# First layer about the mean, for batches 1 to 3: GpSimd products and VectorE sums in place of one-column TensorE products

## The chip, the cores and the metric

The kernel runs on one core of a Trainium2 chip. The metric is the time of one execution on the device in microseconds (us), lower is better. The core's engines run beside each other, each through its own list of instructions in order: TensorE (PE; its weight loads are shown as PEld), VectorE (DVE), ScalarE (ACT), GpSimd (POOL) and SyncE (SP), which only issues transfers. GpSimd issues transfers too.

## The reference

```python
def _attn_ref(q, kv, w_sr):                 # q (4, 12288, 128), kv (4, 384, 32, 128)
    kv_pool = kv.reshape(B, H // 4, 4, W // 4, 4, C).mean(axis=(2, 4))
    kv_flat = kv_pool.reshape(B, -1, C) @ w_sr          # 768 keys, k = v
    s = (q @ kv_flat.transpose(0, 2, 1)) / np.sqrt(C)
    a = np.exp(s - s.max(-1, keepdims=True))
    a /= a.sum(-1, keepdims=True) + 1e-09
    return a @ kv_flat

def _moe_ref(x, w_in, w_out):               # x (49152, 128), w_in (128, 2048), w_out (2048, 128)
    h = x @ w_in
    return (h - np.tanh(h)) @ w_out
```

The attention's output, 4 batches of 12288 tokens, is the x of the second function. Everything is fp32.

## The kernel before

**Rounds.** Each batch has 24 *rounds* of 512 tokens, so there are 96, numbered from 0; each has the same work. The hidden layer is developed about one point for each batch: the mean of its keys times w_sr (the *centre*). The point's own hidden values are worked out once for each batch, and the rounds then carry only each token's distance from the centre.

In a round TensorE issues 3 pairs of scores (L850), 3 pairs of values (L894), 2 sums of the softmax shares (L878, `x<-rs,share`; this one is used below as the mark of a round), 3 products for the linear term of q (L884) and 3 for that of the distance (L954), 8 pairs of the hidden layer (L965, `big<-dr,winr`) and 8 pairs back into the result (L1003, `acc<-r,Wr`). Each of the 8 results in `big` is turned into a cube. For seven, ScalarE squares (L969) and VectorE multiplies (L972). For the eighth ScalarE copies it (L976), and GpSimd makes the cube by three instructions over 128x1024: z+ (L979), z* (L983, `z<-z,v`) and rp (L983, `rp<-z,v`). The last pair back of each round is the one from rp (L1003, `acc<-rp,Wr`). ScalarE takes the three exponentials (L854), VectorE multiplies them (L857). GpSimd also rounds the distance (dr L908) and its rest (dl L934), the rest of q (ql L888), and issues two adding transfers (L873) that sum three tiles r into rs, from which L878 reads.

**Preparing a later batch.** While a batch runs, the next is prepared between its instructions. The names below are those of the code. First 15 adding transfers from GpSimd (*gathers*, L437; one more, the first, comes from SyncE) pool the batch's keys into one tile kvp (128x768). VectorE sums kvp in six parts (L502) and makes the mean of them (L506, L507). ScalarE subtracts the mean (L511); TensorE makes the centre, one column (L514), VectorE copies it to `col` (L517). Then `first(n)`, for n from 0 to 3, is four products of a 128x128 block of the fp32 weights with that column (L614, `x<-col,win`), and `take_first(n)` on VectorE copies the four columns into `hb` (L619), which holds a number for each of the 2048 hidden units as 128x16. From hb GpSimd works out three chains of small instructions: first order (L639 to L646), slopes (L650 to L656), third order (L665 to L670). After these come the scaled weights of the batch, all on GpSimd: winr (L714, 4 instructions of 128x512), Wr (L776, 4) and Wg (L756, 4), and one small instruction each for Mh and Ah. On TensorE there are also the products of keys and values (L521, L530), a moment (L547) and four blocks of slopes (L763, `x<-Wg,wout`). The batch 0 is prepared before its first round, with the same functions in other forms.

**The order.** Every instruction of every engine is put in order ahead of time by a class `Plan`: it walks a clock, and on each engine issues what is ready in the order of a *step* (8 steps are a round), using a rough cost for each instruction. The table `MOVES` shifts the steps of single pieces of the preparation, the table `AT` sets those of the pieces of a round. The costs set only the order; the chip then runs it in that order, each engine waiting where an operand or a buffer is not ready. Buffers are rings by tag: `kc` has 2 (used for keys, then for the scales of winr), `A` has 2, `rs` has 3, `rp` 2.

## Time and profile before

| | us |
|---|---|
| three runs | 1289.19, 1290.86, 1291.06 |
| median | 1290.86 |
| the profiled execution's own time | 1289.32 |
| its span (first to last instruction) | 1287.6 |
| busy share | PE 98%, DVE 94%, ACT 93%, POOL 89% |

The profile is of one execution: its span is that from the first instruction to the last. A row of the timeline has the start, the time from issue to end, the engine, line, tiles, shape and count, and in brackets how long the engine stood idle before it and what it waited for. Where instructions of an engine overlap (TensorE's always, GpSimd's when they are queued), what one of them costs is the distance from start to start, not the second column.

### The profile page before, as it was taken

To read this page: it belongs to the slowest core of one execution; us is meant where nothing else is said; L and a number is where in the kernel's file an instruction comes from. 1 tells how busy PE (TensorE), PEld (TensorE's weight loads), DVE (VectorE), ACT (ScalarE), POOL (GpSimd) and SP (SyncE) were. 2 spreads that over 40 slices of the span, in tenths; PEclk is the share of its full clock that TensorE was granted. 3 is DMA by queue.
4 is the path that set the end of the run, shared out by engine and by line. 5 is a ranking of instruction groups with operands and counts; after the bars stand their busy time and mean duration, and the time that the engine had idled before them with its cause. 6 is when DMAs were issued, how large, how long until landed. Compare 5 with 4: busy or idle time off the path is not lost.

```text
span 1287.6 us, 17375 instructions
## 1 busy us (share of the span) xinstructions
PE 1257.1 (98%) x5520; PEld 879.8 (68%) x5520; DVE 1213.7 (94%) x1201; ACT 1201.0 (93%) x1423; POOL 1147.5 (89%) x969
## 2 busy tenths in 40 slices
PE   5899999999999999999999999999999999999997
PEld 4666667777676677777766667776776666666665
DVE  6899899999999999999999999999999999999996
ACT  4799999999999999999999999999999999999995
POOL 3599987999999988899999987899988988989886
PEclk8999999999999999999999999999999999999999
DMA  9367744456657543455467743444434444344431
GB/s 364 69 144 151 167 98 107 111 127 148 143 132 161 120 118 90 125 131 138 108 148 143 160 103 103 103 119 107 115 90 115 103 106 118 93 115 103 106 88 33
DMA packets 82708, 158.46 MB, mean 123 GB/s; under 512 B 9937, under 2 KB 12113, under 8 KB 82609
## 3 DMA queue, kind: packets, MB, share of 16 engines
q0 software_dynamic: 33552, 66.99, 30.7%
q1 hardware_dynamic: 49056, 90.29, 20.0%
q8 instruction: 45, 0.74, 0.2%
q14 instruction: 55, 0.44, 0.1%
HBM read 57.93 MB, written 25.39 MB: 65 GB/s over the span
## 4 chain that ended last, share of the span: by engine, by line
PE 74%; POOL 14%; DMA 4%; issue 2%; DVE 2%; ACT 2%; SPq 0%; POOLq 0%; ACTq 0%; DVEq 0%
PE big L965 23%; PE acc L1003 22%; PE big L850 8%; PE x L894 8%; PE acc L954 4%; PE x L884 4%; DMA rs<-r 3%; POOL rp L983 3%; PE x L878 3%; POOL z L983 2%; POOL z L979 2%; POOL rs L873 2%; POOL ql L888 1%; POOL dl L934 1%; DVE r L972 1%
## 5 line engine op out<-in xcount | busy, mean ns | idle before, releaser
L972 DVE SCALAR_TENSOR_TENSOR r<-big,u 128x1024 fp32r<-128x1024 f32 x672 | 788.7, 1218 | 26.8 <-ACT u L969 26.4
L969 ACT ACTIVATE u<-big 128x1024 f32<-128x1024 f32 x672 | 671.1, 1029 | 34.8 <-PE big L965 23.3
L965 PE MATMUL big<-dr,winr 128*128 128x512 f32 x1536 | 518.9, 419 | 0.7 <-DVE r L972 0.6
L1003 PE MATMUL acc<-r,Wr 128*128 128x512 f32 x1344 | 414.5, 398 | 0.6 <-DVE r L972 0.6
L857 DVE SCALAR_TENSOR_TENSOR r<-E,big 128x1024 f16<-128x1024 f32 x288 | 350.2, 1217 | 22.5 <-ACT E L854 21.8
L965 PEld LDWEIGHTS big<-dr,winr 128*128 128x128 f32 x1536 | 272.1, 188 | 118.8 <-DVE r L972 33.0
L854 ACT ACTIVATE E<-big 128x1024 f32<-128x1024 f32 x288 | 297.2, 1033 | 3.7 <-PE big L850 2.5
L1003 PEld LDWEIGHTS acc<-r,Wr 128*128 128x128 f32 x1344 | 250.0, 188 | 58.5 <-DVE r L972 1.5
L983 POOL TENSOR_TENSOR rp<-z,v 128x1024 fp32r<-128x1024 f32 x96 | 270.8, 2821 | 0.2
L983 POOL TENSOR_TENSOR z<-z,v 128x1024 f32<-128x1024 f32 x96 | 243.8, 2539 | 0.1
L873 POOL DMA_DIRECT2D rs<-r x188 | 211.2, 1124 | 7.6 <-DMA rs<-r 6.1
L979 POOL TENSOR_SCALAR z<-v 128x1024 f32<-128x1024 f32 x96 | 122.7, 1278 | 82.1 <-ACT v L976 81.8
L850 PE MATMUL big<-qr,kTr 128*128 128x512 f32 x576 | 193.0, 417 | 0.4 <-ACT winr L746 0.2
L888 POOL TENSOR_TENSOR ql<-q,qr 128x512 fp32r<-128x512 f32 x96 | 185.2, 1929 | 1.1 <-ACT qr L835 1.1
L894 PE MATMUL x<-r,vvr 128*128 128x512 f16 x576 | 174.3, 385 | 0.0
L934 POOL TENSOR_TENSOR dl<-df,dr 128x512 fp32r<-128x512 f32 x96 | 163.2, 1700 | 0.0
L850 PEld LDWEIGHTS big<-qr,kTr 128*128 128x128 f32 x576 | 101.4, 188 | 39.9 <-DVE r L972 21.9
L976 ACT COPY v<-big 128x1024 f32<-128x1024 f32 x96 | 97.5, 1016 | 8.1 <-PE big L965 1.6
L894 PEld LDWEIGHTS <-vvr 128*128 128x128 f16 x576 | 33.4, 98 | 78.6 <-issue 78.4
L908 POOL TENSOR_SCALAR dr<-df 128x512 fp32r<-128x512 f32 x96 | 81.4, 848 | 0.0
L1003 PE MATMUL acc<-rp,Wr 128*128 128x512 f32 x192 | 77.0, 482 | 3.6 <-POOL rp L983 3.6
L1014 ACT ACTIVATE o<-acc,At 128x512 f32<-128x512 f32 x96 | 65.6, 683 | 7.5 <-PE acc L1003 7.4
(184 smaller groups left out, 1029.9 us busy)
## 6 DMA issues: line engine op xcount, KB each, us to landing
rs<-r POOLq DMA_DIRECT2D x188, 256.0 KB, 3.6
q<-in_q_dram SPq DMA_DIRECT2D x96, 256.0 KB
out_dram<-o SPq DMA_DIRECT2D x96, 256.0 KB
rs<-r SPq DMA_DIRECT2D x94, 256.0 KB
kvp<-in_kv_by_place_dram POOLq DMA_DIRECT2D x45, 384.0 KB, 6.0
r<-in_kv_by_key_dram SPq DMA_DIRECT2D x6, 512.0 KB
kc<-inverse SPq DMA_DIRECT2D x12, 256.0 KB
u<-in_moe_w_in_dram SPq DMA_DIRECT2D x3, 512.0 KB
```

Source lines behind the costliest of these rows:

```text
L850: PE.matmul(out=half(plan[s], h), lhsT=plan[kTr][:, n * P : (n + 1) * P], rhs=plan[qr], start=True, stop=True)
L854: A.activation(out=plan[e], in_=plan[s], func=AF.Exp)
L857: V.scalar_tensor_tensor(out=plan[r], in0=plan[e], scalar=-1.0, in1=plan[s], op0=ALU.add, op1=ALU.subtract)
L873: PL.dma_start(out=plan[rs], in_=plan[r2s[k]], accum_op=ALU.add)
L888: PL.tensor_tensor(out=plan[ql], in0=plan[qs], in1=plan[qr].bitcast(F32), op=ALU.subtract)
L894: PE.matmul(out=plan[num], lhsT=plan[vvr][:, n], rhs=half(plan[f"r2.{g}.{k}"], h), start=(start and h == 0), stop=(stop and h == 1))
L934: PL.tensor_tensor(out=plan[dl], in0=plan[df], in1=plan[dr].bitcast(F32), op=ALU.subtract)
L965: PE.matmul(out=half(plan[hp], h), lhsT=plan[winr][:, f * P : (f + 1) * P], rhs=plan[dr], start=True, stop=True)
L969: A.activation(out=plan[u], in_=plan[hp], func=AF.Square)
L972: V.scalar_tensor_tensor(out=plan[r], in0=plan[hp], scalar=1.0, in1=plan[u], op0=ALU.add, op1=ALU.mult)
L983: PL.tensor_tensor(out=plan[to], in0=plan[x], in1=plan[y], op=ALU.mult)
L1003: PE.matmul(out=plan[acc], lhsT=plan[Wr][:, 2 * n + h], rhs=half(plan[r], h), start=(start and h == 0), stop=(stop and h == 1))
```

## The change

For the batches 1 to 3:

- The centre is made in another form: a product of 128x128 with the mean broadcast as weights, so that every partition holds the whole centre; ScalarE scales it into a tile of tag `A`.
- `first(n)` is one GpSimd product, 128x512: the transposed weights of four blocks by the centre, into a tile of tag `kc`. `take_first(n)` is a sum on VectorE over 128 columns, four times (128x4x128 to 128x4).
- The keys' mean is one sum on VectorE over 768 columns in place of six partial ones and a sum.
- The planner's cost of a gather and of an adding transfer goes from 0.88 and 0.9 to 0.62, their delays to landing from 2.3 and 1.43 to 2.5 and 1.5. The tables MOVES (now with nearly every piece of the preparation, and new entries `taken` for take_first) and AT have new numbers throughout.

```diff
     MOVES = {
-        "load.i.0": -22.9, "load.i.1": -18.7, "words.i.1": -54.5, "words.i.3": -7.3, "WW": -172.2,
+        "load.i.0": -587.048, "words.i.0": -199.957, "load.i.1": -193.024, "words.i.1": 138.935,
...
-            plan.op(put - (0.01 if w else 4), *(("POOL", 0.88) if w else ("SP", 0.5)), gather, (), (kvp,),
-                    late=0.81 if w else 1.0, dma=2.3 if w else 1.1)
+            plan.op(put - (0.01 if w else 4), *(("POOL", 0.62) if w else ("SP", 0.5)), gather, (), (kvp,),
+                    late=0.81 if w else 1.0, dma=2.5 if w else 1.1)
...
-        sb(cen, "col", [P, 1])
+        sb(cen, *(("A", [P, C]) if b else ("col", [P, 1])))
...
-            V.tensor_reduce(out=r[:, 24:25], in_=r[:, 0:24], op=ALU.add, axis=AX.X)
+            V.tensor_reduce(out=r[:, 24:25], in_=plan[kvp] if b else r[:, 0:24], op=ALU.add, axis=AX.X)
...
-            PE.matmul(out=plan[pc][:, 0:1], lhsT=wsr, rhs=plan[row][:, 25:26], start=True, stop=True)
+            mean_of = plan[row][:, 25:26]
+            if b:
+                PE.matmul(out=plan[pc][:, 0:P], lhsT=mean_of.to_broadcast([P, P]), rhs=wsr, start=True,
+                          stop=True)
...
+                A.activation(out=plan[cen], in_=plan[pc][:, 0:P], func=AF.Copy, scale=-1.0 / W)
...
-        for n in range(NK // 2):
+        for n in range(0 if b else NK // 2):
...
         def first(n):
-            for k in range(4):
-                f = 4 * n + k
-                at = plan[f"{ph}.{n}"][:, k : k + 1] if b else plan[f"{ph}.0"][:, f : f + 1]
-                PE.matmul(out=at, lhsT=win32[:, f * P : (f + 1) * P], rhs=plan[cen], start=True,
+            if b:
+                by = plan[cen].unsqueeze(1).to_broadcast([P, FT // 4, C])
+                PL.tensor_tensor(out=plan[f"{ph}.{n}"], in0=winT[:, 4 * n : 4 * n + 4], in1=by, op=ALU.mult)
+                return
...
         def take_first(n):
-            to, of = (slice(4 * n, 4 * n + 4), slice(0, 4)) if b else (slice(0, FT),) * 2
-            V.tensor_scalar(out=x(0)[:, to], in0=plan[f"{ph}.{n}"][:, of], scalar1=1.0, scalar2=None,
-                            op0=ALU.mult)
+            if b:
+                V.tensor_reduce(out=x(0)[:, 4 * n : 4 * n + 4], in_=plan[f"{ph}.{n}"], op=ALU.add, axis=AX.X)
...
     AT = dict(
-        forth=[4.5, 6.4, 3.4, 2.2, 5.4, 5.7, 0.3, 2.8],
+        forth=[6.183, 7.436, 3.897, 1.231, 6.907, 6.934, 0.646, 2.941],
...
-                plan.op(s0 + AT["added"][k - 1], "POOL", 0.9, partial(added, k), (r2s[k],), to,
-                        late=0.81, dma=1.43, lane=True)
+                plan.op(s0 + AT["added"][k - 1], "POOL", 0.62, partial(added, k), (r2s[k],), to,
+                        late=0.81, dma=1.5, lane=True)
```

In the order of before, TensorE has this around the first of the four blocks for batch 2 (L514 makes the centre, L614 are the one-column products):

```order
L1003 MATMUL acc_5000<-r_4942,Wr_2762 128x512 x2
L514 MATMUL x_5030<-row_4601,wsr_66 128x1
L965 MATMUL big_5032<-dr_4883,winr_3208 128x512 x2
L1003 MATMUL acc_5000<-r_4957,Wr_2762 128x512 x2
L614 MATMUL x_5043<-col_5037,win32_67 128x1 x4
L1003 MATMUL acc_5000<-r_4981,Wr_2762 128x512 x2
L965 MATMUL big_5057<-dr_5023,winr_3208 128x512 x2
```

In the order of after (L1009, L1047, L998 are the lines of before 965, 1003, 954) TensorE has for the same batch only the centre, L542:

```order
L998 MATMUL acc_5651<-dl_5599,Ah_3906 128x512
L1009 MATMUL big_5661<-dr_5535,winr_3156 128x512 x2
L1047 MATMUL acc_5651<-r_5580,Wr_2620 128x512 x2
L1009 MATMUL big_5672<-dr_5535,winr_3156 128x512 x2
L1047 MATMUL acc_5651<-r_5591,Wr_2620 128x512 x2
L1009 MATMUL big_5682<-dr_5535,winr_3156 128x512 x2
L1047 MATMUL acc_5651<-r_5608,Wr_2620 128x512 x2
L542 MATMUL x_5689<-wsr_66,row_4310 128x128
L1047 MATMUL acc_5651<-r_5632,Wr_2620 128x512 x2
L1009 MATMUL big_5697<-dr_5670,winr_3156 128x512 x2
```

Four blocks like the first are gone from TensorE for each of three batches, and nothing has come in their place there.

GpSimd in the order of before, in the round in which the first chain of batch 2 runs (the chain starts at L639):

```order
L983 TENSOR_TENSOR z_5572<-z_5572,v_5559 128x1024
L873 DMA rs_5555<-r2_5581 128x1024
L983 TENSOR_TENSOR rp_5622<-z_5572,v_5559 128x1024
L934 TENSOR_TENSOR dl_5647<-df_5574,dr_5585 128x512
L873 DMA rs_5555<-r2_5561 128x1024
L888 TENSOR_TENSOR ql_5674<-q_5234,qr_5470 128x512
L639 TENSOR_TENSOR hb_5060<-hb_5060 128x16
L640 TENSOR_SCALAR hb_5060<-hb_5060 128x16
```

In the order of after, GpSimd has the products (L649) of batch 2 in these places (L1023, L952, L1027, L917, L978, L932 are 979, 908, 983, 873, 934, 888 of before; L679 starts the first chain):

```order
L932 TENSOR_TENSOR ql_5757<-q_5331,qr_5558 128x512
L649 TENSOR_TENSOR kc_5770<-winT_68,A_5695 128x512
L1023 TENSOR_SCALAR z_5809<-v_5796 128x1024
L952 TENSOR_SCALAR dr_5822<-df_5811 128x512
L1027 TENSOR_TENSOR z_5809<-z_5809,v_5796 128x1024
L649 TENSOR_TENSOR kc_5850<-winT_68,A_5695 128x512
L649 TENSOR_TENSOR kc_5858<-winT_68,A_5695 128x512
L649 TENSOR_TENSOR kc_5868<-winT_68,A_5695 128x512
L917 DMA rs_5792<-r2_5827 128x1024
L1027 TENSOR_TENSOR rp_5889<-z_5809,v_5796 128x1024
L679 TENSOR_TENSOR hb_5816<-hb_5816 128x16
L680 TENSOR_SCALAR hb_5816<-hb_5816 128x16
```

Three of the four products stand between z* and the adding transfer and rp of one round (round 39; for batch 3 it is round 63, in the same pattern; for batch 1 all four stand in round 12), and the first chain follows rp there.

GpSimd early in batch 0, where the gathers (L437) for batch 1 run, in the order of before:

```order
L437 DMA kvp_342<-in_kv_by_place_dram 128x768
L873 DMA rs_1020<-r2_1048 128x1024
L983 TENSOR_TENSOR rp_1100<-z_1041,v_1026 128x1024
L934 TENSOR_TENSOR dl_1127<-df_1039,dr_1052 128x512
L437 DMA kvp_342<-in_kv_by_place_dram 128x768
L873 DMA rs_1020<-r2_1028 128x1024
L888 TENSOR_TENSOR ql_1165<-q_716,qr_937 128x512
L979 TENSOR_SCALAR z_1178<-v_1161 128x1024
```

And in that of after (L463 is the gather):

```order
L917 DMA rs_744<-r2_770 128x1024
L1027 TENSOR_TENSOR rp_809<-z_761,v_748 128x1024
L978 TENSOR_TENSOR dl_838<-df_763,dr_774 128x512
L917 DMA rs_744<-r2_750 128x1024
L932 TENSOR_TENSOR ql_859<-q_295,qr_661 128x512
L463 DMA kvp_312<-in_kv_by_place_dram 128x768
L1023 TENSOR_SCALAR z_897<-v_884 128x1024
```

Before had two gathers in each of four early rounds, each gather ahead of one of the round's adding transfers; after has one a round there, behind the last of them, and doubles only later.

## Rows read from the trace of the kernel before

**Rows 1.** The page's busy times; columns: us, share of the span, instructions.

```profile
PE 1257.1 (98%) x5520; PEld 879.8 (68%) x5520; DVE 1213.7 (94%) x1201; ACT 1201.0 (93%) x1423; POOL 1147.5 (89%) x969
```

**Rows 2.** Timeline of TensorE, 1100 to 1128: start, time, instruction, [idle, releaser].

```profile
1112.19 0.60 PE L878 MATMUL x<-rs,share 128*128 128x512 f16 x2
...
1115.35 0.82 PE L1003 MATMUL acc<-rp,Wr 128*128 128x512 f32 x2
...
1124.51 0.61 PE L878 MATMUL x<-rs,share 128*128 128x512 f16 x2
```

**Rows 3.** Timeline of TensorE, 459 to 487, a block of products for batch 2.

```profile
473.19 0.60 PE L878 MATMUL x<-rs,share 128*128 128x512 f16 x2
...
483.13 0.95 PE L614 MATMUL x<-col,win 128*128 128x1 f32 x8
...
486.35 0.61 PE L878 MATMUL x<-rs,share 128*128 128x512 f16 x2
```

**Rows 4.** Groups by line: count | busy us, mean ns | idle.

```profile
L502 DVE TENSOR_REDUCE row<-kvp 128x4 f32<-128x128 f32 x24 | 6.3, 276 | 2.5 <-POOL kvp L460 2.5
...
L466 DVE TENSOR_REDUCE kvp<-E 128x64 f32<-128x1024 f32 x2 | 2.4, 1214 | 0.0
...
L732 POOL TENSOR_TENSOR Wg<-ident,hb 128x512 f32<-128x512 f32 x2 | 2.1, 1042 | 4.9 <-ACT E L854 4.9
...
L732 DVE TENSOR_TENSOR Wg<-ident,hb 128x512 f32<-128x512 f32 x2 | 1.3, 682 | 0.0
...
L619 DVE TENSOR_SCALAR hb<-x 128x4 f32<-128x4 f32 x12 | 1.8, 151 | 0.0
```

**Rows 5.** Timeline of GpSimd, 600 to 640, among winr, Wr and a gather.

```profile
613.71 2.87 POOL L983 TENSOR_TENSOR z<-z,v 128x1024 f32<-128x1024 f32 x1
...
622.20 2.61 POOL L714 TENSOR_TENSOR winr<-win,kc 128x512 fp32r<-128x512 f32 x1
623.70 1.96 POOL L437 DMA_DIRECT2D kvp<-in_kv_by_place_dram  x1
...
626.83 2.85 POOL L983 TENSOR_TENSOR z<-z,v 128x1024 f32<-128x1024 f32 x1
...
636.82 2.07 POOL L776 TENSOR_TENSOR Wr<-wout,hb 128x512 fp32r<-128x512 f32 x1
637.83 2.07 POOL L979 TENSOR_SCALAR z<-v 128x1024 f32<-128x1024 f32 x1
...
639.99 2.87 POOL L983 TENSOR_TENSOR z<-z,v 128x1024 f32<-128x1024 f32 x1
```

**Rows 6.** Timeline of GpSimd, 526 to 560, the slopes chain.

```profile
535.72 0.20 POOL L650 TENSOR_SCALAR hb<-hb 128x16 f32<-128x16 f32 x1
...
537.76 1.04 POOL L756 TENSOR_TENSOR Wg<-winT,hb 128x512 f32<-128x512 f32 x1
```

**Rows 7.** Timeline of GpSimd, 1100 to 1126, no preparation left.

```profile
1111.39 2.67 POOL L983 TENSOR_TENSOR rp<-z,v 128x1024 fp32r<-128x1024 f32 x1
...
1119.06 1.05 POOL L979 TENSOR_SCALAR z<-v 128x1024 f32<-128x1024 f32 x1 [1.60 <-ACT v L976]
```

**Rows 8.** Timeline of TensorE, 523 to 541, the products of keys for batch 2.

```profile
524.94 0.60 PE L878 MATMUL x<-rs,share 128*128 128x512 f16 x2
...
539.80 0.60 PE L878 MATMUL x<-rs,share 128*128 128x512 f16 x2
```

**Rows 9.** Waits of all engines: us in total, times, longest.

```profile
PEld acc L1003 <- POOL rp L983: 7.9, 12, 1.6
```

**Rows 10.** Timeline of GpSimd, 110 to 154, two gathers in a round.

```profile
123.59 1.20 POOL L437 DMA_DIRECT2D kvp<-in_kv_by_place_dram  x1
...
137.24 1.19 POOL L437 DMA_DIRECT2D kvp<-in_kv_by_place_dram  x1
```

**Rows 11.** Timeline of TensorE, 48 to 62, ahead of the first round's hidden layer.

```profile
57.90 2.05 PE L763 MATMUL acc<-Wg,wout 128*128 128x129 f32 x16 [0.70 <-DVE wout L355]
59.70 1.19 PE L965 MATMUL big<-dr,winr 128*128 128x512 f32 x4
```

More of the change, by code (lines that the diff above doesn't have):

```diff
@@ L610, in first @@
         def first(n):
-            for k in range(4):
-                f = 4 * n + k
-                at = plan[f"{ph}.{n}"][:, k : k + 1] if b else plan[f"{ph}.0"][:, f : f + 1]
-                PE.matmul(out=at, lhsT=win32[:, f * P : (f + 1) * P], rhs=plan[cen], start=True,
+            if b:
+                by = plan[cen].unsqueeze(1).to_broadcast([P, FT // 4, C])
+                PL.tensor_tensor(out=plan[f"{ph}.{n}"], in0=winT[:, 4 * n : 4 * n + 4], in1=by, op=ALU.mult)
+                return
+            for f in range(4 * n, 4 * n + 4):
+                PE.matmul(out=plan[f"{ph}.0"][:, f : f + 1], lhsT=win32[:, f * P : (f + 1) * P], rhs=plan[cen], start=True,
                           stop=True)
         def take_first(n):
-            to, of = (slice(4 * n, 4 * n + 4), slice(0, 4)) if b else (slice(0, FT),) * 2
-            V.tensor_scalar(out=x(0)[:, to], in0=plan[f"{ph}.{n}"][:, of], scalar1=1.0, scalar2=None,
-                            op0=ALU.mult)
+            if b:
+                V.tensor_reduce(out=x(0)[:, 4 * n : 4 * n + 4], in_=plan[f"{ph}.{n}"], op=ALU.add, axis=AX.X)
+            else:
+                V.tensor_scalar(out=x(0), in0=plan[f"{ph}.0"][:, 0:FT], scalar1=1.0, scalar2=None,
+                                op0=ALU.mult)
         def x(n):
@@ L672, in about_centre @@
         for n in range(4):
-            plan.op(first_at[n], "PE", 0.9, partial(first, n), (cen, ("win32", n)),
-                    (f"{ph}.{n}" if b else (f"{ph}.0", n),), late=0.2)
             if b:
-                plan.op(first_at[n], "DVE", 0.17, partial(take_first, n), (f"{ph}.{n}",), ((hb, n),))
+                plan.op(first_at[n], "POOL", 1.05, partial(first, n), (cen, "winT"), (f"{ph}.{n}",))
+            else:
+                plan.op(first_at[n], "PE", 0.9, partial(first, n), (cen, ("win32", n)), ((f"{ph}.0", n),),
+                        late=0.2)
+            if b:
+                plan.op(at(first_at[n] + 0.5, "taken", c, n), "DVE", 0.62, partial(take_first, n), (f"{ph}.{n}",), ((hb, n),))
         if not b:
@@ L806, in attention_then_ffn @@
     AT = dict(
-        forth=[4.5, 6.4, 3.4, 2.2, 5.4, 5.7, 0.3, 2.8],
-        first=[3.7, 6.2, 2.3, -0.8, 5.0, 5.8, -1.2, 1.38],
-        then=[-4.8, 10.1, 6.0, 3.7, 9.5, 10.0, 2.4, 5.4],
-        back=[11.5, 11.0, 7.1, 6.3, 10.16, 10.3, 5.6, 6.46], scores=[-20.8, -19.0, -20.4],
-        exps=[-22.6, -20.0, -21.2], beyond=[-18.5, -15.0, -17.6], values=[-4.7, -4.5, -3.3],
-        more=[-2.2, -1.7], num=-5.0, copied=16.8, added=[-26.1, -22.4], shares=-5.6, left=-8.4,
-        straight=-3.6, apart=-0.6, rounded=-11.8, rounded_q=-25.5, slope=5.0, result=10.5,
-        lower_q=-21.6, lower_left=-6.6)
+        forth=[6.183, 7.436, 3.897, 1.231, 6.907, 6.934, 0.646, 2.941],
+        first=[6.113, 7.386, 5.163, 2.701, 6.659, 7.002, 0.664, 4.618],
+        then=[-4.052, 8.093, 3.114, 0.965, 6.316, 6.82, 0.535, 1.349],
+        back=[12.167, 11.017, 7.582, 7.301, 8.805, 10.879, 6.918, 7.459],
+        scores=[-20.726, -17.216, -19.822], exps=[-19.243, -17.524, -18.238],
+        beyond=[-22.476, -19.463, -19.757], values=[-4.358, -3.915, -1.404], more=[-3.22, -0.014],
+        num=-4.806, copied=-5.69, added=[-27.038, -22.755], shares=-5.473, left=-4.337,
+        straight=-1.917, apart=-3.508, rounded=-12.048, rounded_q=-23.422, slope=6.851,
+        result=13.55, lower_q=-20.071, lower_left=-7.159)
     def attention(g, s0):
```

15 lines of the change are left out of this document (10 added, 5 removed), and 58 rows, old and new, of the table MOVES.

## The prediction

> **What bounds the kernel now.** I read the page's busy shares first: TensorE is at 98%, VectorE at 94%, GpSimd at 89% [rows 1]. Everything is nearly full, so a gain on TensorE is worth only what the others can follow. Then TensorE's timeline where no preparation is left. From one L878 to the next is 12.32 us [rows 2], and in this stretch its instructions stand end to end: I take 12.3 us as its own time for a round. VectorE's 94% leaves it some 0.7 us of such a round. GpSimd I read from start to start where it is queued. From z* to z* is 13.16 us with one winr (1.50 us) and one Wr (1.01 us) between [rows 5]. Without these a round is 10.65 us. The round before it, 13.12 us, holds a winr and a gather [rows 5], so a gather is about 0.97 us. GpSimd therefore has 12.3 - 10.65 = 1.65 us to give in each round, and everything for the next batch must go into that. Where nothing is prepared it does stand idle for 1.60 us ahead of z+ [rows 7], and its rp, done at 1111.39 + 2.67 = 1114.06, is used by TensorE's pair at 1115.35 [rows 2, 7], 1.3 us later. So TensorE notices a GpSimd that falls behind only after a lead of 1.6 us has been used up, or 2.9 us if the 1.3 can be used as well. It notices even now: the weight load of that pair waited 12 times for rp, 7.9 us in all [rows 9].
>
> **The change, part by part.**
>
> *Products off TensorE.* A round with one block of one-column products goes from 473.19 to 486.35, which is 13.16 us against 12.3 [rows 3], so a block costs 0.86 us on the engine that is full. There are four for each of three batches: 12 x 0.86 = 10.3 us come off TensorE. The centre as 128x128 is one instruction more or less of the same order for each batch, and ScalarE's copy of it lies in an engine with 7% idle [rows 1]: nothing.
>
> *Products onto GpSimd.* No row shows this product; the nearest is Wg, 128x512 on GpSimd at 1.04 us, and Wr's 1.01 from start to start [rows 4, 5]. I take 1.0 us, so 12 us in all, 4 for each batch. A second bound, if GpSimd runs it as VectorE ran the same form, is 0.68 us [rows 4], 8 us in all. The row of Wg shows GpSimd slower than VectorE by 1042/682 = 1.5 for one form of instruction. The Trainium skill, "GPSIMD Engine Reference", section 4.1 (Engine selection), speaks against the change: it gives products of two tiles to VectorE and calls GpSimd about twice slower for them. By this page the price would be 2 x 0.68 = 1.4 us, an estimate, and 16 us in all; the trace shows 1.5 times, not 2.
>
> *What of it lies on the path.* In the order of after I counted what GpSimd has in each round, and weighed it against TensorE. Small instructions of a chain are 2.04/7 = 0.29 us each [rows 6]. The blocks of slopes stay, also four at a time, and I price them like the blocks of products, 0.86.
> Rounds 14 to 22: 9 x 10.65, 7 gathers (6.8), 4 winr (6.0), 4 Wr (4.0), 2 Wg (2.0), 13 small ones (3.8): 118.5 us. TensorE: 9 x 12.3 and 2 blocks of slopes (1.7): 112.4. GpSimd is 6.1 short.
> Rounds 39 to 46: 8 x 10.65, 3 products (3.0), 21 small ones (6.1), 4 winr (6.0), 4 Wg (4.0), 2 Wr (2.0), 4 gathers (3.9), Mh (0.4, an estimate): 110.6. TensorE: 8 x 12.3, keys' work 2.6 (a round with keys' products was 539.80 - 524.94 = 14.86 [rows 8]), 3 blocks of slopes (2.6): 103.6. Short by 7.0.
> Rounds 63 to 69: 7 x 10.65 and the same extras without the gathers, 96.1, against 7 x 12.3, keys' work and 2 blocks of slopes, 90.4: short by 5.7.
> Together 18.8 us. From each of the three a lead of 1.6 to 2.9 us goes off, which leaves 10.1 to 14.0. I take 12 us. In the order of before the same count never uses up the lead in these stretches: the blocks on TensorE gave GpSimd the time. Of the three causes here (the products themselves, TensorE's shorter rounds, the preparation drawn closer together) the trace of before can't part them.
>
> *Sums on VectorE.* take_first goes from a copy of 0.15 us to a sum over 512 columns. A sum over 1024 takes 1.21 us [rows 4], so I take 0.6. The six parts at 0.28 each [rows 4] give way to one sum over 768, about 0.9. For a batch: 4 x 0.45 + 0.9 - 1.7 = 1.0 us more. It lies in the 0.7 us a round that VectorE has to give, save where three sums stand close to one another: I take 0.4 a batch, 1.1 us in all; bounds 0 and 3.
>
> *Gathers moved.* Before, two gathers stand in each of four early rounds, each ahead of an adding transfer. From gather to gather over such a round is 137.24 - 123.59 = 13.65 us [rows 10], 1.3 more than 12.3. After has one there, behind the last transfer, which fits into 1.65 us of idle time: I take -2.8 us (of 4 x 1.3 at most, as two of the rounds are milder). Later batches have more double rounds than before (24 to 26, 49, 51 to 53): +2.3 us by the same price less the lead. What else of the 7.9 us of waits for rp [rows 9] lies in the preparation of before and is counted anew in my 12 us: -1.2 us.
>
> *The start.* TensorE issues the last slopes of batch 0 at 57.90, after a wait of 0.70 us, and the first hidden layer at 59.70 [rows 11]. After has the first hidden pairs ahead of those slopes: 1.8 and part of the wait, about -2.3 us. Bounds: -4 (more of the start moves with it) and +1.5 (exponentials now stand ahead of the copies of winr on ScalarE).
>
> The sum: -10.3 + 12 + 1.1 - 2.8 + 2.3 - 1.2 - 2.3 = **-1.2 us**. Against the profiled execution's own 1289.32 that is 1288.1. The median of the three runs is 1290.86, 1.54 above it; on that scale the forecast is 1289.6, said as **1289.5 us**.
>
> **The rivals.**
>
> *A. GpSimd doesn't bind.* The planner's tables may have put rp early enough, or the 1.3 us ahead of the pair and the rings of r and rp may give more lead than I allow, so that the shortfall is bridged from the idle time of the rounds after. For it: in the trace of before full rounds of GpSimd stand at 13.1 us [rows 5] without a wait in most of them. Against it: three stretches in a row of 7 to 9 rounds are above TensorE's time, and a lead is used only once. It gives the sum without the 12: 1289.6 - 12 = 1277.6; 1272 to 1285.
>
> *B. Slower: VectorE is held by GpSimd's products.* The sums stand at fixed places in VectorE's order, three in the round of three products, and behind each stand the cubes that TensorE waits for. There are two kc buffers: the fourth product waits for the second sum, and each sum for its product. If GpSimd comes into rounds 12, 39 and 63 over some 1 us late, VectorE stops at a sum, the cubes behind it come late, and GpSimd, whose z+ needs ScalarE's copy of a later pair, is held in turn. The price is about the three products that then lie open, 3 us for each batch: +9, 1298.6; 1294 to 1303. For it: the three products stand ahead of rp and an adding transfer. Against it: GpSimd has its full lead when these rounds begin, as nothing but gathers stands before.
>
> *C. VectorE sets the round.* If VectorE can't go below the rounds it had with a block of products, TensorE's 0.86 doesn't come back, and GpSimd's shortfall is hidden under it too: about 1290.9, 1289 to 1293. Its 94% speaks against it [rows 1].
>
> By the rule of the Trainium skill (section 4.1 of that page), GpSimd would be 16 - 12 = 4 us more in debt, which gives 1293.5: that lies in the forecast's case.
>
> **How the numbers follow.** The forecast, what TensorE saves is paid back by GpSimd, has 0.42, with 1285 to 1294 as its own range. A has 0.28, B 0.25, C 0.05. A run of this kernel can't be told from no change within 0.2%, 2.6 us: 1288.3 to 1293.4. Below that lie nearly all of A (0.265) and 0.125 of the forecast: 0.39. Within it 0.24 of the forecast, 0.045 of C and 0.025 of the edges of A and B: 0.31. Above it 0.24 of B, 0.055 of the forecast and the rest of C: 0.30. The range goes from 1276 to 1300: it leaves out some 0.11 of A below and 0.08 of B above.
>
> **What the profile of after would show.** Products gone: rounds at 12.3 us where blocks stood, up to round 11 and from 28 to 37. GpSimd's debt: in rounds 14 to 22, 39 to 46 and 63 to 69 no idle time on GpSimd, rounds of 12.9 us and more, and waits of the pair of rp (L1047) for rp of some 12 us in all beside those early in the run. If these waits are under 4 us and the rounds are 12.3, A is right. If VectorE's sums (L657) wait for GpSimd by over 1 us, B is. A product at 1.0 us from start to start shows the price right. The first hidden layer should start near 57.5. I am wrong in the main if GpSimd's time for a round isn't a sum of its parts, or if a full GpSimd round may be late by more than 2.9 us without TensorE waiting.

## The result, and the profile after

The change made the kernel slower: 1302.47 us (1300.47 to 1305.22) against 1290.62 us before, a ratio of 1.0095 (95% interval 1.0075 to 1.0116). The forecast was 1289.5 us with a range of 1276 to 1300; it gave 0.39 to a time clearly below that of before, 0.31 to no visible change and 0.30 to a slower kernel. The profiled execution after took 1305.22 us, 2.75 above its median; its span is 1303.5 us. The runs below were made on four chips, on which the kernel before had medians of 1290.89 to 1291.6 us.

The page of after, busy times and the chain that ended last (the work that ended last, followed back through what released it); behind it the chain of before:

```profile
PE 1257.1 (96%) x5424; PEld 872.2 (67%) x5424; DVE 1218.8 (94%) x1180; ACT 1204.5 (92%) x1426; POOL 1162.5 (89%) x981
PE 53%; POOL 31%; DMA 6%; issue 4%; DVE 3%; ACT 2%; SPq 0%; POOLq 0%; ACTq 0%
```

```profile
PE 74%; POOL 14%; DMA 4%; issue 2%; DVE 2%; ACT 2%; SPq 0%; POOLq 0%; ACTq 0%; DVEq 0%
```

The shares of busy time say almost nothing: GpSimd stays at 89% [rows 1]. The chain says it: the share of GpSimd on it goes from 14% to 31%. The waits of after say for what:

```profile
PEld acc L1047 <- POOL rp L1027: 26.0, 33, 2.1
...
POOL rs L917 <- DMA rs<-r: 12.3, 13, 1.7
PE acc L1047 <- POOL rp L1027: 11.1, 21, 1.6
PEld big L1009 <- POOL dr L952: 9.2, 11, 2.7
...
DVE hb L657 <- POOL kc L649: 2.0, 5, 0.6
```

The wait of the last pair's weight load for rp goes from 7.9 us in 12 [rows 9] to 26.0 in 33, and one is nearly new: the hidden layer's weight loads wait for dr, 9.2 us against 0.2 before. VectorE's sums wait for the products only 2.0 us.

What the change took off TensorE did come off. The marks of two rounds in which before had a block of products (13.16 us there [rows 3]) now lie 12.27 us apart:

```profile
490.89 0.60 PE L922 MATMUL x<-rs,share 128*128 128x512 f16 x2
...
503.16 0.60 PE L922 MATMUL x<-rs,share 128*128 128x512 f16 x2
```

Where the time went is read from the end of ScalarE's result in each round, one trace against the other. Rounds are counted here by these results, from 0; GpSimd's rounds as the prediction counts them are two ahead, so that its round 39 falls into the time of result 37 and the end of its round 46 into that of 45. The first line of the table is after less before at the end of the given round; the second is the same for a pair of runs (g_after, g_before, below) in which the transfers of the gathers are nearly taken away.

| result of round | 0 | 8 | 17 | 26 | 36 | 48 | 60 | 71 | 95 |
|---|---|---|---|---|---|---|---|---|---|
| after - before, us | +1.6 | +1.9 | -0.1 | +7.4 | +2.2 | +11.2 | +10.6 | +15.8 | +15.8 |
| g_after - g_before, us | -0.2 | +0.1 | -2.2 | +3.5 | -1.6 | +7.4 | +3.0 | +8.0 | +8.1 |

In the pair without the gathers' bytes it falls by 5.1 and 4.4 us where before had the blocks (26 to 36, 48 to 60; some 1.2 of each is keys' work that after does a round later), and rises by some 9 and 5 in the rounds behind, where the products, the chains and the scaled weights stand on GpSimd. The two profiled executions differ by 15.8 us in the results, 4 more than the medians: the first pair has a late start in after and slower rounds with gathers. In the second pair traces (8.1) and medians (8.2) agree.

### The profile page after: what moved, and what is told of

The parts are those of the page before. It is cut to its first block, busy times and chain, and to the rows that moved or that the text cites. A ratio compares the mean times of both kernels' runs of the same rounds, so it can differ in the third digit from the quotient of the medians.

```text
span 1303.5 us, 17190 instructions
## 1 busy us (share of the span) xinstructions
PE 1257.1 (96%) x5424; PEld 872.2 (67%) x5424; DVE 1218.8 (94%) x1180; ACT 1204.5 (92%) x1426; POOL 1162.5 (89%) x981
## 4 chain that ended last, share of the span: by engine, by line
PE 53%; POOL 31%; DMA 6%; issue 4%; DVE 3%; ACT 2%; SPq 0%; POOLq 0%; ACTq 0%
PE big L1009 16%; PE acc L1047 16%; POOL rp L1027 6%; POOL z L1027 6%; PE x L938 6%; PE big L894 6%; DMA rs<-r 4%; POOL rs L917 4%; POOL z L1023 4%; PE x L928 3%; PE acc L998 3%; POOL ql L932 3%; POOL dl L978 2%; PE x L922 2%; POOL kvp L463 1%
## 5 line engine op out<-in xcount | busy, mean ns | idle before, releaser
L1013 ACT ACTIVATE u<-big 128x1024 f32<-128x1024 f32 x672 | 672.0, 1030 | 34.9 <-PE big L1009 22.8
L1009 PE MATMUL big<-dr,winr 128*128 128x512 f32 x1536 | 503.6, 409 | 6.8 <-POOL dr L952 4.3
L1047 PE MATMUL acc<-r,Wr 128*128 128x512 f32 x1344 | 429.7, 411 | 0.6 <-DVE r L1016 0.6
L1009 PEld LDWEIGHTS big<-dr,winr 128*128 128x128 f32 x1536 | 272.1, 188 | 124.1 <-DVE r L1016 31.6
L1047 PEld LDWEIGHTS acc<-r,Wr 128*128 128x128 f32 x1344 | 251.1, 188 | 64.8 <-DVE r L1016 1.5
L1027 POOL TENSOR_TENSOR rp<-z,v 128x1024 fp32r<-128x1024 f32 x96 | 272.1, 2835 | 0.2
L1027 POOL TENSOR_TENSOR z<-z,v 128x1024 f32<-128x1024 f32 x96 | 244.8, 2550 | 0.1
L917 POOL DMA_DIRECT2D rs<-r x188 | 210.5, 1120 | 18.0 <-DMA rs<-r 12.3
L1023 POOL TENSOR_SCALAR z<-v 128x1024 f32<-128x1024 f32 x96 | 123.8, 1289 | 71.8 <-ACT v L1020 71.7
L932 POOL TENSOR_TENSOR ql<-q,qr 128x512 fp32r<-128x512 f32 x96 | 181.8, 1894 | 3.7 <-ACT qr L879 3.7
L978 POOL TENSOR_TENSOR dl<-df,dr 128x512 fp32r<-128x512 f32 x96 | 164.7, 1716 | 0.0
L1047 PE MATMUL acc<-rp,Wr 128*128 128x512 f32 x192 | 75.4, 474 | 11.3 <-POOL rp L1027 11.1
L1058 ACT ACTIVATE o<-acc,At 128x512 f32<-128x512 f32 x96 | 65.8, 685 | 18.6 <-PE acc L1047 17.6
L952 POOL TENSOR_SCALAR dr<-df 128x512 fp32r<-128x512 f32 x96 | 82.0, 854 | 0.2 <-DVE df L949 0.2
```

Of the source, the lines that this page charges most:

```text
L917: PL.dma_start(out=plan[rs], in_=plan[r2s[k]], accum_op=ALU.add)
L932: PL.tensor_tensor(out=plan[ql], in0=plan[qs], in1=plan[qr].bitcast(F32), op=ALU.subtract)
L978: PL.tensor_tensor(out=plan[dl], in0=plan[df], in1=plan[dr].bitcast(F32), op=ALU.subtract)
L1009: PE.matmul(out=half(plan[hp], h), lhsT=plan[winr][:, f * P : (f + 1) * P], rhs=plan[dr], start=True, stop=True)
L1013: A.activation(out=plan[u], in_=plan[hp], func=AF.Square)
L1027: PL.tensor_tensor(out=plan[to], in0=plan[x], in1=plan[y], op=ALU.mult)
```

## The experiments

Theory G: the products' own time on GpSimd is paid back on the path. Theory T: the new tables draw GpSimd's other work together, and the products matter little. Each ratio is against the kernel before on the same chip.

**Cut the products (e3b_small).** The changed kernel in its order:

```diff
-PL.tensor_tensor(out=plan[f"{ph}.{n}"], in0=winT[:, 4 * n : 4 * n + 4], in1=by, op=ALU.mult)
+PL.tensor_tensor(out=plan[f"{ph}.{n}"][:, :, 0:4], in0=winT[:, 4 * n : 4 * n + 4, 0:4], in1=by[:, :, 0:4], op=ALU.mult)
...
-    with tc.If(ok == 0, label="any"):
+    with tc.If(ok == 2, label="any"):
```

VectorE's sums read one column again and again and keep their length; the second edit keeps the kernel on its fast path.

> The run with cut products again (each of the 12 GpSimd products 128x4x4 in place of 128x4x128, sums on VectorE unchanged in length, the changed kernel's own order), now with the branch to the general path taken out, so that the fast path is what is timed. It leaves out the first layer about the mean, so the values are not those of the reference. Theory G (the products' own time on GpSimd is what is paid back): about 1.0 us back for each of 12, of which 9 to 12 show: 1290 to 1294 us against 1302.5. Theory T (the tables draw GpSimd's other work together, the products matter little): 1299 to 1303.

1300.33 us, ratio 1.0076 (1.0051 to 1.0101): about 2 us off by the medians, which is not clear of noise (after's ratio was 1.0095, 1.0075 to 1.0116), and far from the 9 to 12 of theory G. (A first run without the second edit took the kernel's general path, 25361 us, since the cut values fall out of the range that the kernel tests; it says nothing.) The products after, and cut, from the groups by line:

```profile
L649 POOL TENSOR_TENSOR kc<-winT,A 128x512 f32<-128x512 f32 x12 | 17.6, 1551 | 0.0
```

```profile
L649 POOL TENSOR_TENSOR kc<-winT,A 128x16 f32<-128x16 f32 x12 | 4.4, 414 | 4.0 <-DVE hb L657 4.0
```

GpSimd has 13 us less of products and waits 4.0 us for VectorE between them instead. Round by round the traces show more than the medians: rounds are shorter by 1.3 us in 11, by 0.5, 0.2 and 0.7 in 37 to 39, by 0.5, 0.2 and 0.7 in 61 to 63, and by 1.0 in 45, where TensorE's granted clock stays at 1.00 this time; in sum some 5 us, as 40 to 44 stay nearly as they were. What GpSimd saves in its round 39 it can't carry on whole: it stands idle 2.90 us ahead of a z+ (1.79 in after), which needs ScalarE's copy of a pair that TensorE hasn't issued yet:

```profile
546.35 1.05 POOL L1023 TENSOR_SCALAR z<-v 128x1024 f32<-128x1024 f32 x1 [2.90 <-ACT v L1020]
```

So the products' own time is worth 2 to 5 us. Theory G fell at its price. Of theory T the half stood that the products' time matters little; that the tables are to blame this run doesn't show.

**Cut the gathers' transfers (g_after, g_before).**

```diff
-PL.dma_start(out=plan[kvp], in_=kv_by_place[b - 1, w], accum_op=ALU.add)
+PL.dma_start(out=plan[kvp][:, 0:32], in_=kv_by_place[b - 1, w][:, 0:32], accum_op=ALU.add)
```

> The changed kernel in its own order, with each of the 45 gathers on GpSimd cut to 32 of 768 columns, and the branch to the general path taken out. It leaves out most of the keys of batches 1 to 3, so the values are not those of the reference. GpSimd still issues every gather. If the bytes of the gathers are what makes rs late and the bunched rounds long (24 to 26, 49 to 53, 5 to 8): 5 to 9 us off, 1294 to 1298. If it is GpSimd's own time (issue 0.6 to 0.97 us each, in rounds already full): 0 to 3 off.

> The same cut of the gathers in the kernel before, in its own order, as the measure for g_after. Before lost some 4 to 5 us in rounds 3 to 6 and about 1.5 in later rounds with gathers: 1284 to 1287 if the bytes are the cause, 1288 to 1291 if GpSimd's issue is. The difference between this gain and that of g_after is what the new places of the gathers cost in transfers.

1292.18 us (ratio 1.0005, 0.9995 to 1.0016) and 1284.01 us (0.9944, 0.9928 to 0.9960). The bytes cost before some 7 us (as expected) and after some 10 (5 to 9 expected). So of the 11.85 us of the change, 1292.18 - 1284.01 = 8.2, on one chip, have nothing to do with the gathers' bytes, and 3.7 come from their new places. In g_after no engine waits for rs any more, and GpSimd's rp still makes TensorE wait:

```profile
PEld acc L1047 <- POOL rp L1027: 16.7, 26, 2.0
PEld big L1009 <- POOL dr L952: 8.9, 10, 2.7
```

```profile
PEld acc L1003 <- POOL rp L983: 3.9, 7, 1.4
```

The first two are of g_after, the last of g_before.

**An instruction more, where GpSimd is idle and where it is full (d1_idle, d2_full, d3_after_full).** Nothing is moved; ql is written twice:

```diff
-            PL.tensor_tensor(out=plan[ql], in0=plan[qs], in1=plan[qr].bitcast(F32),
-                             op=ALU.subtract)
+            for _ in range(2 if g in (77, 78, 79, 80, 81, 82, 83, 84, 85, 86, 87, 88) else 1):
+                PL.tensor_tensor(out=plan[ql], in0=plan[qs], in1=plan[qr].bitcast(F32),
+                                 op=ALU.subtract)
```

> The kernel before, its order unchanged, with one GpSimd instruction of 1.25 us more (ql, written a second time with the same value, as long as one of the new products) in each of 12 rounds without preparation, 76 to 87, where GpSimd stood idle 1.6 us a round. If GpSimd's idle time takes an instruction at no cost: 0 to 0.5 us. If it costs wherever it stands (z+ and rp later by 1.25 us each round): up to 15 us, 1291 to 1306.

> The same 12 instructions of 1.25 us in the kernel before, its order unchanged, but in rounds 41 to 46 and 63 to 68, where winr, Wr, Wg and gathers stand. By my count GpSimd is then 84.1 us against TensorE's 77.7 in the first six and 84.0 against 78.6 in the second: short by 6.4 and 5.4. With the lead of 1.6 to 2.9 us that the prediction took off each stretch: 6 to 9 us slower, 1297 to 1300. If no lead can be saved up, each round paying for itself: 11 to 14 us slower, 1302 to 1305.

> The changed kernel, its order unchanged, with the same instruction twice in each of the nine rounds 18 to 26, which ran at 13.1 us and more. If GpSimd sets these rounds: 9 x 1.25 = 11 us more, 1312 to 1315. If something else does (transfers, VectorE): 0 to 5 us.

1292.78 us (1.0007, 0.9992 to 1.0023), 1306.52 us (1.0112, 1.0087 to 1.0137) and 1316.99 us (1.0191, 1.0165 to 1.0217; 14.5 above after). The same 12 instructions cost nothing that can be told from noise in one place (-1 to 3 us) and 15 us in the other. In the trace of d1_idle eleven of the twelve rounds are as long as before, to 0.02 us; the twelfth, in which 13 small instructions fill GpSimd ahead of z+, is 1.3 us longer, and there TensorE waits:

```profile
1100.20 0.73 PE L966 MATMUL big<-dr,winr 128*128 128x512 f32 x2 [0.60 <-POOL dr L909]
```

GpSimd in an idle round (d1_idle), and in a full one (d2_full):

```profile
1107.35 3.25 POOL L889 TENSOR_TENSOR ql<-q,qr 128x512 fp32r<-128x512 f32 x2
1110.57 1.06 POOL L980 TENSOR_SCALAR z<-v 128x1024 f32<-128x1024 f32 x1
```

```profile
628.06 3.54 POOL L889 TENSOR_TENSOR ql<-q,qr 128x512 fp32r<-128x512 f32 x2
631.55 1.58 POOL L714 TENSOR_TENSOR winr<-win,kc 128x512 fp32r<-128x512 f32 x1
```

The second writing cost more than I had set: 3.22 - 1.25 = 2.0 us in the one, 3.49 - 1.25 = 2.2 in the other (the second starts 0.08 us after the first has ended). So d2_full doesn't tell "lead" from "no lead" as I had meant. With the mean cost in its trace, 2.05 and 1.93 us, GpSimd is short by 11.2 and 9.5 us in the two stretches, an estimate from the count of the expectation; the results are 7.8 us later over rounds 40 to 47 and 6.0 over 61 to 69. About 3.5 us of each were swallowed: a lead is there in the order of before, somewhat more than the 1.6 to 2.9 that I took off. In d3_after_full the nine cost GpSimd 18.6 us, and rounds 17 to 25 of the results are 11.9 us longer in sum, each by 0.9 to 1.8: there most of GpSimd's time sets the round, though not all.

**The pile in round 46 (x45_later).**

```diff
-"third.2.0": -396.162,
+"third.2.0": 40,
...
-"third.2.1": -171.307,
+"third.2.1": 40,
```

> The changed kernel with two numbers of MOVES changed (third.2.0 and third.2.1 to 40): the second Wr of round 46, which stood with a gather, the third chain and another Wr ahead of z+ and dr, comes a round later, and for batch 3 two Wr move from round 69 to 70. The pile in round 46 made one round of 16.2 us in which TensorE waited 2.3 us for dr. If that pile is what costs: this round falls by 1.0 us and the wait for dr with it, to 13.5 to 15, in all 1.5 to 3 us off, 1299.5 to 1301. If GpSimd's work only moves to the next round: 0.

1305.39 us (1.0107, 1.0082 to 1.0132): the gain that was expected is not in the time, which is a miss; rounds with gathers differ by up to 0.4 us each from one trace of this order to another. What the move did shows in the rounds. After, GpSimd, then TensorE, then the granted clock in a table of stretches (busy of PE, PEld, DVE, ACT, POOL, then PEclk, DMA, GB/s):

```profile
655.71 1.96 POOL L463 DMA_DIRECT2D kvp<-in_kv_by_place_dram  x1
656.34 1.59 POOL L705 TENSOR_SCALAR hb<-hb 128x16 f32<-128x16 f32 x1
...
659.47 2.04 POOL L819 TENSOR_TENSOR Wr<-wout,hb 128x512 fp32r<-128x512 f32 x2
661.48 1.05 POOL L1023 TENSOR_SCALAR z<-v 128x1024 f32<-128x1024 f32 x1
662.49 0.62 POOL L952 TENSOR_SCALAR dr<-df 128x512 fp32r<-128x512 f32 x1
```

```profile
663.16 1.22 PE L1009 MATMUL big<-dr,winr 128*128 128x512 f32 x2 [2.28 <-POOL dr L952]
664.18 1.05 PE L1047 MATMUL acc<-r,Wr 128*128 128x512 f32 x2
665.04 1.05 PE L1009 MATMUL big<-dr,winr 128*128 128x512 f32 x2
```

```profile
663.00:664.00 1.00, 0.83 (x2) 0.74 (x3) 0.00 (x0) 0.00 (x0) 1.00 (x2) 0.51 0.00 0
664.00:665.00 1.00, 1.00 (x3) 0.75 (x3) 0.00 (x0) 0.58 (x1) 1.00 (x1) 0.50 0.00 0
665.00:666.00 1.00, 1.00 (x4) 0.44 (x3) 0.52 (x1) 0.45 (x1) 1.00 (x2) 0.50 0.00 0
667.00:672.00 5.00, 5.00 (x23) 3.36 (x23) 4.43 (x4) 4.91 (x7) 5.00 (x5) 1.00 0.57 122
```

A gather, six small instructions and two Wr stand ahead of z+ and dr; TensorE stands idle 2.28 us, and then its granted clock is 0.5 of full speed (the 1.2 GHz level) for some 3 us: pairs start 0.86 to 1.02 us apart where it is 0.46 else. From the first pair behind the wait to the next scores it is 668.01 - 663.16 = 4.85 us:

```profile
668.01 0.62 PE L894 MATMUL big<-qr,kTr 128*128 128x512 f32 x2
```

That round is 16.21 us. In x45_later one Wr less stands there:

```profile
660.37 0.73 PE L999 MATMUL big<-dr,winr 128*128 128x512 f32 x2 [1.29 <-POOL dr L942]
...
663.71 0.62 PE L884 MATMUL big<-qr,kTr 128*128 128x512 f32 x2
```

The wait is 1.29, the granted clock stays at 1.00, no pair behind it is slow, and the same way takes 663.71 - 660.37 = 3.34 us: the low clock cost some 1.5. The round is 14.22. 1.0 us moved on GpSimd took 2.0 off, of which 1.1 came back in rounds 47 to 49. For batch 3 the same move gave 1.1 in one round and took 1.3 in the next: nothing.

**Products on GpSimd, placed otherwise (b1_even, b2_one).** In the changed kernel three of four products wait for a kc buffer which the values of the batch hold until their moment (L581, round 39). b1_even has before's tables, and the products ahead of the values:

```diff
-        sb(vv32, "kc", [P, KT, C])
+        sb(vv32, "kc", [P, KT, C], step=-1e6 + 10 * b + 2)
...
-                sb(f"{ph}.{n}", "kc", [P, FT // 4, C])
+                sb(f"{ph}.{n}", "kc", [P, FT // 4, C], step=-1e6 + 10 * b + 1)
...
-                sb(ir, "kc", [P, P // 2, FT])
+                sb(ir, "kc", [P, P // 2, FT], step=-1e6 + 10 * b + 3)
...
-        sb("all_left", "kc", [P, B, N // P])
+        sb("all_left", "kc", [P, B, N // P], step=0.0)
```

with the steps of the mean lower by 8 (batch 1) and 16, those of the products by 16 and 24.

> The changed code with the tables and costs of the kernel before, but the products given the kc buffers ahead of the batch's values (in the changed kernel three of four products wait for a buffer that the moment of the values frees), the mean one to two rounds earlier and the products two to three rounds earlier. GpSimd then has two products a round in rounds 31 and 32 (55 and 56), where it stood idle 1.6 us a round, and the chains follow one a round. Theory G (a product costs only where GpSimd has no time left): TensorE's 10.3 us come back nearly whole, 1280 to 1285. If GpSimd's products cost wherever they stand, or VectorE's sums set the round: 1289 to 1295.

1288.20 us, ratio 0.9972 (0.9962 to 0.9982): a little faster than before and 14 us faster than after. The same products that stand in the slower kernel cost little here. The run e1_oldtables below has the same code and costs and, but for these steps, the same tables, with the products behind the values: 1311.79 us on the same chip. So with these tables the place of the products, and of what follows them, is worth 23.6 us. But only a quarter of TensorE's 10.3 us is seen, and VectorE has most of the rest: the two rounds with two sums are 1.1 and 1.5 us above 12.3, of some 3.4 that TensorE saves in the batch. VectorE and TensorE in a round with two sums:

```profile
469.35 0.69 DVE L629 TENSOR_REDUCE hb<-kc 128x4 f32<-128x512 f32 x1 [0.46 <-POOL kc L621]
470.55 0.67 DVE L629 TENSOR_REDUCE hb<-kc 128x4 f32<-128x512 f32 x1
```

```profile
472.41 0.74 PE L980 MATMUL big<-dr,winr 128*128 128x512 f32 x2 [1.32 <-DVE r L872]
```

The two rounds (30, 31) are 13.40 and 13.75 us.

> As the run b1_even, but the planner's cost of a product is 1.9 in place of 1.05, so that it puts one product, and one sum on VectorE, into each of four rounds (30 to 33, 54 to 57, 10 to 13) in place of two, and the mean is another round earlier for batches 2 and 3. In b1_even the rounds with two sums of 0.7 us were 13.4 to 13.8 us, with TensorE waiting for VectorE. If VectorE's spare 0.4 to 0.7 us a round is what limits: the rounds with one product fall to 12.3 to 12.7 and the whole to 1282 to 1286. If GpSimd's 1.24 us for a product is what costs, even where it stood idle: no gain over b1_even, 1287 to 1290.

b2_one, with a planner's cost of 1.9 for a product: 1299.97 us (1.0068, 1.0054 to 1.0082), a miss. Its rounds with one product and one sum are 12.6 us:

```profile
460.56 0.61 PE L893 MATMUL x<-rs,share 128*128 128x512 f16 x2
...
473.13 0.61 PE L893 MATMUL x<-rs,share 128*128 128x512 f16 x2
```

but the higher cost pushed the last winr of batch 1 past the batch's end, and one round took 25.1 us:

```profile
PE big L980 <- POOL winr L729: 9.9, 1, 9.9
```

So what sums cost on VectorE is shown (13.6 us for a round with two, 12.6 with one, 12.3 with none); a gain by spreading them isn't.

**The mean alone (m1_mean).** Before with only the three edits for the keys' mean.

> The kernel before with only the keys' mean by one sum over 768 columns in place of six partial sums and one sum; tables and products as before. VectorE saves 6 x 0.2 and adds 0.9 for each batch: nothing on the path, 1290 to 1291.5. If the single sum of 0.9 us delays the cubes behind it: up to +0.5 us a batch, 1292.

1293.76 us, 1.0018 (1.0009 to 1.0028), 1.2 to 3.6 us slower than before, where nothing, or up to 1.5, was expected. In its trace one round a batch is 13.1 us (the sum) in place of three of 12.47 (the parts), and the round behind, with the first block, is 0.3 longer: 0.65 us each for batches 2 and 3, 0.8 for batch 1, 2.1 in all, which is what the time shows. So the one sum is a loss by itself: 0.94 us on VectorE in one piece cost more than six parts of 0.28. The rest of the 4.3 us of this trace lies in rounds with gathers, and one run's trace doesn't say why.

**Tables and code taken apart (e1_oldtables, e2_oldcode, e4_costs, e6_start).**

> The changed code for the first layer, the centre and the mean, with the tables and costs of the kernel before. In its order the products of batch 1 stand four in round 16, and round 17 holds the chains, Wg, Wr and gathers of three rounds, 22.8 us of GpSimd; rounds 39, 40 and 45 hold 16, 13.6 and 19.4. Theory G with a lead of 1.6 to 2.9 us: TensorE saves 10.3, GpSimd's lumps cost 15 to 20: 1296 to 1301. If only the new tables are to blame: 1281 to 1286.

> The code of the kernel before (products in TensorE's one-column form) with the new costs and the new tables, save the steps of the first layer and of the keys for batches 1 to 3, which stay as before. Theory T (tables are to blame): the start, the late double gathers and the drawn-together scalings remain, 1298 to 1304. Theory G: GpSimd has 5 us less for each batch, the lumps left are 2 to 5 us in all, and the start 1.6: 1292 to 1297.

> The changed kernel with the planner's costs of gathers and adding transfers as before (0.88 and 0.9 in place of 0.62), which lets the planner see nearly what the trace shows of them (0.6 to 0.97 from start to start); tables and code as changed. Its order has the chains and Wr one or two rounds later and fewer rounds above 13 us of GpSimd: if the too low costs make the debt, 1293 to 1299; if the tables do it whatever the costs, 1300 to 1305.

> The changed kernel with the table entries of batch 0 (loads, first keys, first layer of batch 0) as in the kernel before, the rest as changed. The first result came at 81.05 us after the change and at 79.43 before. If the new entries of the start are the cause: first result near 79.4 and the whole 1.6 us shorter, about 1301. If the start is held by the new table of the rounds (AT), which stays: no change at the first result, 1302 to 1303.

1311.79 us (1.0156, 1.0133 to 1.0179), 1347.43 us (1.0426, 1.0399 to 1.0452), 1328.72 us (1.0294, 1.0277 to 1.0312) and 1311.14 us (1.0153, 1.0136 to 1.0170): all worse than both kernels, and outside what either theory gave. Each has rounds of 17 to 27 us, where an instruction that comes too late stops an engine with everything behind it. In e1_oldtables TensorE waits 7.1 us for a Wg that stands at the end of the 22.8 us pile on GpSimd; in e2_oldcode 9.3 us for Ah at the change of batch; in e4_costs and e6_start VectorE comes to the keys' mean before the last gather has landed. That wait in e4_costs, with TensorE behind it:

```profile
PE x L542 <- DVE row L533: 11.7, 1, 11.7
...
DVE row L532 <- DMA kvp<-in_kv_by_place_dram: 8.0, 1, 8.0
```

They show that the tables and the code belong together. They don't tell how much of the 11.85 us is the tables' alone, and that stays open. e6_start has its first result at 80.57 us, but four traces that keep after's order have it between 79.17 and 81.05, so this run doesn't tell what sets it.

**Products and sums on VectorE alone (v2_vector).**

```diff
-                PL.tensor_tensor(out=plan[f"{ph}.{n}"], in0=winT[:, 4 * n : 4 * n + 4], in1=by, op=ALU.mult)
+                for f in range(4 * n, 4 * n + 4):
+                    V.tensor_tensor_reduce(out=junk, in0=winT[:, f], in1=plan[cen], scale=1.0, scalar=0.0,
+                                           op0=ALU.mult, op1=ALU.add, accum_out=x(0)[:, f : f + 1])
```

> The new centre and the single sum for the mean, with the tables and costs of the kernel before, and the products taken by VectorE alone: 16 instructions a batch that multiply 128x128 and sum the columns at once. So neither TensorE nor GpSimd has them. Theory G: TensorE's 10.3 us come back and GpSimd owes nothing more than before; VectorE's 16 x 0.2 us lie in its spare 0.4 to 0.7 us a round: 1280 to 1285. If VectorE sets the period in those rounds: 1288 to 1292.

1353.05 us, 1.0479 (1.0462 to 1.0497). I had set 0.2 us for one:

```profile
L624 DVE CUSTOM_DVE_ANT_0 junk<-winT,A 128x128 f32<-128x128 f32 x48 | 56.9, 1185 | 1.2
L624 DVE DVE_READ_ACCUMULATOR2_ANT hb<- 128x1 f32 x48 | 3.8, 79 | 0.0
```

1.26 us for each of 48 is 60.7 us on VectorE; the kernel is 62 us longer.

## Why the prediction was wrong, point by point

**TensorE's 10.3 us: right.** Rounds at 12.27 us in place of 13.16.

**GpSimd's debt: the mechanism right, the term mis-sized.** I counted 6.1, 7.0 and 5.7 us for the three batches, 18.8, and took a lead off to get 12. In the pair without gathers' bytes, each batch's difference in the table is 3.5 - 0.1 = 3.4, 7.4 - 3.5 = 3.9 and 8.0 - 7.4 = 0.6. Each batch saves 3.4 us on TensorE there, and 0.2, 0.5 and 0.5 by VectorE's parts that are gone; rounds 26 and 53 hold the one sum for the mean, 0.84 each. With the savings added and the sum taken out, some 6.2, 7.8 and 3.8 us were paid: 18, where I had 12 (what VectorE's sums of the products cost is in it, as no run parts them from GpSimd there).

The count was nearly right. From z* to z* over the three stretches GpSimd took 118.7, 112.7 and 96.8 us, where I had 118.5, 110.6 and 96.1:

```profile
229.86 2.87 POOL L1027 TENSOR_TENSOR z<-z,v 128x1024 f32<-128x1024 f32 x1
...
348.55 2.86 POOL L1027 TENSOR_TENSOR z<-z,v 128x1024 f32<-128x1024 f32 x1
...
866.53 2.38 POOL L1027 TENSOR_TENSOR z<-z,v 128x1024 f32<-128x1024 f32 x1
...
963.28 2.39 POOL L1027 TENSOR_TENSOR z<-z,v 128x1024 f32<-128x1024 f32 x1
```

Against my 112.4, 103.6 and 90.4 for TensorE that is short by 21.7 us, 2.9 more than counted. Of these about 18 were paid, so the lead took off some 4 us and not 6.8, and in the first batch next to nothing (6.3 short, 6.2 paid). The step that failed is the lead, 2.3 us taken off each stretch from the idle time of rounds without preparation. d2_full shows that the order of before could swallow 3.5 a stretch; why the new order swallows less isn't shown. One cost is seen that I didn't have, TensorE's clock at half speed behind a long wait, some 1.5 us in the one round of 16.2. The products and z* in GpSimd's rounds 39 to 47:

```profile
550.42 2.38 POOL L1027 TENSOR_TENSOR z<-z,v 128x1024 f32<-128x1024 f32 x1
552.76 3.78 POOL L649 TENSOR_TENSOR kc<-winT,A 128x512 f32<-128x512 f32 x3
556.49 0.83 POOL L917 DMA_DIRECT2D rs<-r  x1
...
603.64 0.88 POOL L917 DMA_DIRECT2D rs<-r  x1 [1.55 <-issue]
...
644.91 2.27 POOL L1023 TENSOR_SCALAR z<-v 128x1024 f32<-128x1024 f32 x1
...
647.27 2.86 POOL L1027 TENSOR_TENSOR z<-z,v 128x1024 f32<-128x1024 f32 x1
...
663.07 2.38 POOL L1027 TENSOR_TENSOR z<-z,v 128x1024 f32<-128x1024 f32 x1
```

From z* to z* over the eight rounds is 112.65 us, where I had 110.6. A product is 3.73/3 = 1.24 us from start to start, not 1.0, and 1.55 us of idle time stand in it that the profile has no releaser for. By the ratio to VectorE's 0.68 [rows 4] the product is 1.8 times slower. Here the trace is nearer to the Trainium skill ("GPSIMD Engine Reference", section 4.1, Engine selection: "~2× slower for 2-input ops") than to the 1.5 of the row of Wg that I went by.

GpSimd's time also isn't a plain sum, which I had named as a sign of being wrong. z* reads what z+ writes and starts 0.09 us after z+ has ended (644.91 + 2.27 = 647.18; 647.27). From z+ to z* it is 2.36 us in this round, where z+ takes 2.27 us from issue to end, and 1.59 in the next (661.48 to 663.07), where it takes 1.05. My 10.65 us for a bare round hold 0.55 of such a wait: z* starts 2.16 us behind z+ there (637.83 to 639.99 [rows 5]), and the winr that I took out of that round is not in the rows but in this one:

```profile
635.30 2.59 POOL L714 TENSOR_TENSOR winr<-win,kc 128x512 fp32r<-128x512 f32 x1
```

How the 18 us split further is not settled.

That the products themselves are the debt I had left open, and e3b_small answers it: their own time is 2 to 5 us of it. What stands behind them is late: for batch 2 the first chain ends one round later than in before (37 for 36), the second three (39 for 36), the third seven (45 for 38), and the four Wr stand in rounds 45 and 46 in place of 41 to 47, while winr hardly moved. Against before, the pair without gathers' bytes loses 2.3 us in rounds 36 to 39, where the products stand, and 5.6 in 40 to 47; for batch 3 it is 2.2 in 60 to 63 and 1.7 in 64 to 71. That these late chains are the cause is read from the order and not shown by itself; b1_even against e1_oldtables shows with before's tables that an earlier place costs far less, and no run has it with the new tables.

**Gathers: wrong.** I had -2.8 early, +2.3 later, -1.2 for waits of before counted anew: -1.7 together. Measured: +3.7, since cutting the bytes takes 1302.47 - 1292.18 = 10.3 us off after and 6.6 off before. The failed step is to price a gather by GpSimd's issue alone: its bytes cost too, as the cut leaves every issue in place. GpSimd's adding transfers wait 12.3 us for rs in after and not at all in g_after. Early there is no gain: rounds 1 to 8 lose 3.4 us to the bytes in after and 3.3 in before, as the traces with and without them show. Later the loss is larger than I had: 2.4 against 0.4 in rounds 9 to 26, 3.8 against 0.1 in 49 to 60 (these traces lie above the medians).

**The start: wrong.** I had -2.3; the first result came at 81.05 us in this trace, at 81.01, 79.64 and 79.17 in three other runs that keep its order, and at 79.43 before (78.56 to 79.60 in three other runs of before's order). So nothing was gained, and up to 1.6 us lost. The first hidden pairs do stand ahead of the last slopes, but wait for dr, and start at 60.55 against 59.70 [rows 11]:

```profile
60.55 1.21 PE L1009 MATMUL big<-dr,winr 128*128 128x512 f32 x4 [1.03 <-POOL dr L952]
```

**VectorE's sums: probably too small.** I had 1.1 us. The one sum for the mean makes a round a batch 13.1 us (8, 26 and 53), 2.5 us in all, and the parts that are gone give 9 x 0.18 = 1.6 back (rounds of 12.47 in before): +0.9 for the mean alone, and 2.1 in m1_mean. For the sums of the products b2_one shows 0.3 us a round; in after they stand in the rounds of the products, and their share isn't parted.

**The whole.** -10.3 - 1.6 + 2.5 + 18 = +8.6, where the pair without gathers' bytes has 8.2; with 3.7 for the gathers and nothing for the start it is about the 11.85 measured. Against the forecast's -1.2 the debt is 6 us off, the gathers 5.4, the start 2.3.

**The rivals.** B gave nearly the right number (1298.6), by luck. By the sign that I had set for it, sums that wait for GpSimd over 1 us, it shows: 2.0 us. But its price was 9 us at the products, and of what was paid the larger part for batch 2, and nearly half for batch 3, lies behind them. A fell: the waits for rp are 26 us. C fell in this order, with rounds at 12.27 where blocks stood; in b1_even it is seen in part. The end of the range, 1300, was 2.5 us too low: the bounds of gathers and start both lay on the side of a gain.
